# Moving the value-weight cluster, the logits and one eviction in a woven attention and expert kernel

## The chip, the cores and the metric

One core of a Trainium2 chip runs the whole program. The metric is device time in microseconds of one execution; the lower, the better. The profile shows five engines of the core: PE (TensorE, with its weight loads as PEld), DVE (VectorE), ACT (ScalarE), POOL (GpSimd) and SP (SyncE, which here only issues DMAs).

## The reference

Eight batches of eight heads with 576 tokens attend to 32 memory slots per head; the result goes through a mixture of eight experts of which each token uses one.

```
a = softmax(phi, over 32 slots)
k_m = a.T @ k ; v_m = a.T @ v                      per batch and head, 32 x 64
attn = softmax(q @ k_m.T / 8) ; x = attn @ v_m      4608 tokens x 512
logits = x @ w_gate + modality_bias[modality_id]
e = argmax(logits) ; gate = softmax(logits)[e]
out = gate * (relu(x @ w1[e]) @ w2[e])              w1 512 x 1024, w2 1024 x 512
```

## The kernel before, in words

The kernel guesses one expert for all tokens, computes with it, and at the end tests whether any token chose another; only then a general path runs. With the inputs here it doesn't run.

**What is computed per batch b (0 to 7).** `mem_max`, `mem_turn_top`, `mem_swap`, `mem_peak`, `mem_exp`, `mem_sums` (stages `max`, `ttop`, `swap`, `top`, `exp`, `sums`) make the softmax of `phi`; `kv_products` (stage `kv`, L388 and L396 on PE) the memory keys and values, `mem_turn` (stage `kvT`, L146) their transposes `kT` and `vT`. `q_turn` (stage `qt`, four DVE transposes, L552) turns the queries, `scores` (stage `s`, L564) multiplies them with `kT`; with it comes `mem_gate` (L541). `soften` and `normalise` (stages `e` and `n`, DVE with one ACT exp) make the attention weights in two parts, part 0 of 256 tokens and part 1 of 320, and transpose them into `aT`. `a_split` (stages `xu` on ACT and `x` on DVE) splits `aT` into a high and a low half, `xah`/`xal` and `xbh`/`xbl`. `logits` (stage `l`, L683 on PE, `lgT` and `lg` on DVE) and `gate` (stage `g`, L703 to L713 and one ACT exp) make `gates`.

**Value weights.** x @ w1 is never formed as such: `value_products` (L737) multiplies `vT` with the raw `w1`, and `split` (L151 on ACT, L152 on DVE) turns the product into the halves `vwh` and `vwl`. For batches 2 to 7 this is one cluster, `all_value_weights` (stage `vx`): 32 small matmuls into two banks named `pe` and two named `pair`, four casts, four subtractions.

**The two weight layers.** `hidden` (stage `h`, L794) is one of eight chunks f of the hidden layer for one part: six matmuls, then ACT writes `hh` (L807) and DVE `hl` (L811). `outputs` (stage `o`, L830) is one chunk f of one output tile of 128 tokens: three matmuls of 512 columns. Tiles 0 and 1 belong to part 0, tiles 2 and 3 to part 1, and every odd batch ends with a ninth tile for the last 64 tokens of both batches of a pair. After chunk 7, `store` has ACT scale the tile by `gates` into `ob` (L843) and SP store it.

**What sets the order.** Stages are put on two lists, `attention` and `experts`. Each carries its kind (whose cost on PE, DVE, ACT and POOL stands in the table `TAKES`), the stages it comes after, a due time and the PSUM banks it takes. `weave` walks both lists and emits the next attention stage when it is ready and due by the progress of the experts list, else the next expert stage. That order is final on each engine: nothing is reordered later. All tiles named `pe` share a ring of four PSUM banks, taken in turn; a matmul into a bank waits until its last user was read out. In the kernel before, the expert list holds `vx` of the next batch in the middle of the last tile of a batch, and `l` comes after the split of part 1.

Of the kernel before, what the change touches and what calls it, by code (L numbers as in the profile page):

```python
# [54 lines left out]
def attn_moe(ctx: ExitStack, tc: tile.TileContext, q, k, v, phi, mod_id, w_gate, mod_bias, w1, w2, out):  # L55
    nc = tc.nc
    B, H, S, D = q.shape
# [13 lines left out]
    FCH = FF // P  # L71
# [70 lines left out]
    live = {}  # L142
# [729 lines left out]
    def first_w2(c):  # L872
# [7 lines left out]
    attention, experts = [], []  # L880
# [20 lines left out]
    }  # L901


    WORTH = {"h": 0.35, "vw": 0.5, "vx": 0.5, "o": 1.0}
    BATCH = WORTH["h"] * FCH * (0.73 + 0.9) + 4.5 * FCH * 0.693 + WORTH["vw"] * 2.8

    def stage(to, name, kind, after, what, *args, due=-1.0, floor=0.0, banks=0, full=False):

        to.append((name, kind, after, due, floor, lambda: what(*args), banks, full))
# [113 lines left out]
    def plan_steps(b, dues):  # L1025

        free = [[("h", b - 2, part, FCH - 1)] if b > 1 else [] for part in range(2)]
        pair, i = b // 2, b % 2
        todo = []

        def add(name, kind, after, what, *args):
            todo.append((name, kind, after, what, args))

        def step(part):
            for k in range(4):
                before = ("e", b, part, k - 1) if k else ("s", b, part if b == 0 else 0)
                add(("e", b, part, k), f"e{part}{k}", [before], soften, b, part, k)

        def weights(part):
            for k in range(3):  # L1040
                before = [("n", b, part, k - 1) if k else ("e", b, part, 3)]
                if b and k == 2:
                    before += [("l", b - 1), ("x", b - 1, 1)]
                add(("n", b, part, k), f"n{part}{k}", before, normalise, b, part, k)

        def put(part):
            wait = free[part] + ([("w2", FCH - 1)] if b == 0 else [])
            add(("xu", b, part), f"xu{part}", [("n", b, part, 2)] + wait, a_split, b, part, 0)
            add(("x", b, part), f"xl{part}", [("xu", b, part)], a_split, b, part, 1)

        if b:
            add(("s", b, 0), "sg" if b > 1 else "s", [("kvT", b), ("qt", b, HG - 1)], scores_gate if b > 1 else scores, b)
            step(0)
            if b > 1:
                step(1)
            weights(0)
            put(0)
            if b == 1:
                step(1)
        else:  # L1060
            step(1)
            todo.insert(len(todo) - 1, (("vg", 0), "vg", [("e", 0, 1, 0)], mem_gate, (0,)))
        weights(1)
        if b == 0:
            put(1)
        if b < 2:
            add(("l", b), "l", [("n", b, 1, 2), ("vg", b)], logits, b)
        if b:
            put(1)
        if b > 1:  # L1070
            add(("l", b), "lx", [("n", b, 1, 2), ("vx", b)], logits, b)
        c0, n = RA * i, RB if i else RA
        add(("g", b), "g", [("l", b)], gate, pair, c0, n)
        if i:
            add(("others", pair), "others", [("g", b)], others, pair)
            if b < B - 1:
                add(("bias", pair + 1), "nothing", [], biases, pair + 1)
        for (name, kind, after, what, args), due in zip(todo, dues):
            one_bank = int(kind == "sg")
            stage(attention, name, kind, after, what, *args, due=due, banks=one_bank, full=bool(one_bank))  # L1080
        if b == B - 1:
            stage(attention, ("v",), "verdict", [("others", pair)], verdict, due=due + 12.0)

# [7 lines left out]
    def plan_experts(b):  # L1091
        def next_values(hf):
            if b + 1 < B:
                stage(experts, ("vw", b + 1, hf), "vw", [("kvT", b + 1)], value_weights, b + 1, hf, banks=2, full=True)

        def some(t, f, kind, terms):
            last_ = f == FCH - 1 and terms[-1] == 2
            stage(
                experts, ("o", b, t, f, terms[0]), ("o" if last_ else "") + kind, [("g", b)] if last_ else [],
                outputs, t, range(f, f + 1), store(b, t), terms, banks=int(f == terms[0] == 0), full=last_,  # L1100
            )

        def tile_(t):
            for f in range(FCH):
                some(t, f, "o", range(3))

                if b and t == (None if b % 2 else 3) and f == FCH // 2 - 1 and b + 1 < B:
                    stage(experts, ("vx", b + 1), "vw2", [("kvT", b + 1)], all_value_weights, b + 1, banks=2, full=True)
                if b == 0 and t == 3 and f == 1:
                    next_values(0)  # L1110
                if b == 0 and t == 3 and f == FCH - 1:
                    stage(experts, ("vwp", 1, 1), "vwpu", [("kvT", 1)], value_upper_weights, 1, 1, banks=2, full=True)
                    stage(experts, ("vw", 1, 1), "vwl", [("x", 1, 0), ("vwp", 1, 1)], value_lower, 1)
# [26 lines left out]
    def evenly(first, gap, n=24):  # L1140
        return [first + gap * k for k in range(n)]

    AHEAD, SPREAD = (5.8, 5.0), 0.55
    plan_first()
    plan_steps(0, evenly(1.4, 0.25))
    plan_memory(1, 5.9, floor=27.5)
    plan_turns(1, 10.0, 0.9, floor=36.7)
    plan_steps(1, evenly(16.5, 0.5, 10) + evenly(22.5, 0.4))
    for b in range(2, B):
        at0 = (b - 1) * BATCH - AHEAD[b > 2]  # L1150
        plan_memory(b, at0)
        plan_turns(b, at0 + 6.0, 1.3)
        plan_steps(b, evenly(at0 + 11.5, SPREAD, 24))
    for b in range(B):
        plan_experts(b)
    attention.sort(key=lambda s: s[3])
# [1 line left out]
    def weave():  # L1158
# [8 lines left out]
        def ready(s):  # L1167
            if not s or any(n not in done for n in s[0][2]):
                return None


            t = max([0.0] + [done[n] + (0.1 if n[0] != "sums" else -1.2) for n in s[0][2] if n[0] not in ("g", "vx")])
            pe, chain = TAKES[s[0][1]]
            if not pe and chain:

                t -= 0.3
                if t <= free["D" if chain[0] == "T" else chain[0]] or chain[0] == "P":
                    t = 0.0
            t = max(t, s[0][4])
            if s[0][6]:  # L1180
                t = max([t] + [ring[(turn_ + k) % 4] + 0.1 for k in range(s[0][6])])
            return t
# [196 lines left out]
```

## Time and profile before

| | us |
|---|---|
| median of 3 runs | 395.72 (395.28 to 395.73) |
| the profiled execution | 395.99 |
| its span, first to last instruction | 394.1 |
| PE busy | 378.3 (96%) |
| DVE busy | 244.8 (62%) |
| ACT busy | 143.1 (36%) |
| POOL busy | 46.3 (12%) |

The span is what the profile covers; the 1.9 us around it belong to the execution too. Matmuls are pipelined: a matmul of 256 columns shows some 0.28 us, but the next one starts 0.12 us after it, so PE's pace is read from starts, not from durations.

### The profile page before, as it was taken

How to read it: one execution, taken by the hardware profiler on the slowest of the kernel's cores; microseconds unless marked ns; L12 is line 12 of the kernel's file. 1: busy time of each engine (PE TensorE's matmuls, PEld its weight loads, DVE VectorE, ACT ScalarE, POOL GpSimd, SP SyncE). 2: the span in 40 equal slices, each digit the busy share in tenths (PEclk: the TensorE clock that was granted, in tenths of full speed). 3: DMA queues.
4: the chain of work that ended last, by engine and by line, in shares of the span. 5: the costliest groups of instructions: out<-in, count | busy, mean ns of one | idle time of the engine just before them, and what ended most of it. 6: DMA issues, size and time to landing. Idle time of an engine off the chain costs nothing.

```text
span 394.1 us, 10016 instructions
## 1 busy us (share of the span) xinstructions
PE 378.3 (96%) x4158; PEld 307.0 (78%) x4158; DVE 244.8 (62%) x620; ACT 143.1 (36%) x348; POOL 46.3 (12%) x113
## 2 busy tenths in 40 slices
PE   8799999999998999999999999999999999999992
PEld 3577885889767888788977879788887879688982
DVE  4787756895678467664867378674776558560400
ACT  2292524425134333423424333334424325431410
POOL 3247020023000300002000400002000300000000
PEclk9999999999999999999999999999999999999998
DMA  8999349435910493407520292423511011521121
GB/s 299 352 379 362 67 123 377 138 146 137 343 39 28 115 360 119 160 19 264 213 53 28 80 340 109 169 76 98 198 28 39 17 30 27 201 93 30 27 43 47
DMA packets 28844, 56.91 MB, mean 144 GB/s; under 512 B 3060, under 2 KB 8436, under 8 KB 28788
## 3 DMA queue, kind: packets, MB, share of 16 engines
q1 hardware_dynamic: 28368, 55.73, 42.6%
q8 instruction: 35, 0.57, 0.6%
q10 hardware_dynamic: 420, 0.43, 0.3%
q14 instruction: 21, 0.17, 0.1%
HBM read 37.28 MB, written 18.87 MB: 142 GB/s over the span
## 4 chain that ended last, share of the span: by engine, by line
PE 78%; DVE 12%; ACT 4%; DMA 3%; issue 1%; SPq 0%; ACTq 0%
PE pe L830 44%; PE pe L794 22%; PE pair L388 4%; DVE vwl L152 4%; PE pair L564 3%; DMA kv_sb<-in_v_dram 3%; PE pe L737 2%; ACT vwh L151 2%; ACT ob L843 1%; DVE xbl L666 1%; PE pair L737 1%; DVE lgT L690 1%; PE pair L146 1%; PE pe L413 1%; DVE a L603 0%
## 5 line engine op out<-in xcount | busy, mean ns | idle before, releaser
L830 PE MATMUL pe<-w2h,hh 128*128 128x512 f32 x288 | 115.4, 401 | 0.0
L830 PE MATMUL pe<-w2h,hl 128*128 128x512 f32 x288 | 112.4, 390 | 0.0
L830 PE MATMUL pe<-w2l,hh 128*128 128x512 f32 x288 | 110.2, 390 | 0.0
L811 DVE SCALAR_TENSOR_TENSOR hl<-pe,hh 128x256 fp32r<-128x256 f32 (+2 forms) x158 | 56.9, 391 | 30.1 <-ACT hh L807 27.0
L807 ACT ACTIVATE hh<-pe 128x256 fp32r<-128x256 f32 (+2 forms) x158 | 52.4, 363 | 39.8 <-PE pe L794 39.4
L830 PEld LDWEIGHTS pe<-w2h,hh 128*128 128x128 f32 x288 | 54.1, 188 | 12.7 <-issue 1.9
L830 PEld LDWEIGHTS pe<-w2l,hh 128*128 128x128 f32 x288 | 54.0, 188 | 11.7
L830 PEld LDWEIGHTS pe<-w2h,hl 128*128 128x128 f32 x288 | 54.1, 188 | 10.0
L843 ACT ACTIVATE ob<-pe,gates 128x512 f32<-128x512 f32 x35 | 24.0, 688 | 73.7 <-PE pe L830 36.3
L794 PE MATMUL pe<-xbh,vwh 128*128 128x320 f32 x128 | 40.3, 315 | 0.1
L794 PE MATMUL pe<-xah,vwh 128*128 128x256 f32 x124 | 36.2, 295 | 3.7 <-DVE hl L811 2.2
L794 PE MATMUL pe<-xbh,vwl 128*128 128x320 f32 x128 | 39.6, 309 | 0.0
L794 PE MATMUL pe<-xbl,vwh 128*128 128x320 f32 x128 | 39.5, 309 | 0.0
L794 PE MATMUL pe<-xal,vwh 128*128 128x256 f32 x124 | 34.9, 283 | 0.3 <-DVE xal L666 0.3
L794 PE MATMUL pe<-xah,vwl 128*128 128x256 f32 x124 | 34.8, 282 | 0.0
L322 POOL COPY ts<-tm 32x4 f32<-32x4 f32 x24 | 4.8, 200 | 212.2 <-DVE tm L314 211.5
L794 PEld LDWEIGHTS pe<-xah,vwh 128*128 128x128 f32 x124 | 23.6, 191 | 7.5 <-DVE hl L811 2.8
L794 PEld LDWEIGHTS pe<-xbh,vwh 128*128 128x128 f32 x128 | 24.0, 188 | 0.7 <-ACT ob L843 0.4
L794 PEld LDWEIGHTS pe<-xbl,vwh 128*128 128x128 f32 x128 | 24.0, 188 | 0.2
L794 PEld LDWEIGHTS pe<-xal,vwh 128*128 128x128 f32 x124 | 23.6, 191 | 0.8 <-DVE xal L666 0.5
L794 PEld LDWEIGHTS pe<-xbh,vwl 128*128 128x128 f32 x128 | 24.0, 188 | 0.0
L794 PEld LDWEIGHTS pe<-xah,vwl 128*128 128x128 f32 x124 | 23.6, 191 | 0.0
(178 smaller groups left out, 447.7 us busy)
## 6 DMA issues: line engine op xcount, KB each, us to landing
kv_sb<-in_k_dram SPq DMA_DIRECT2D x8, 1152.0 KB, 6.1
kv_sb<-in_v_dram SPq DMA_DIRECT2D x8, 1152.0 KB, 9.2
out_dram<-ob SPq DMA_DIRECT2D x65, 128.0 KB, 2.4
q_sb<-in_q_dram SPq DMA_DIRECT2D x7, 1152.0 KB, 7.9
ph<-in_phi_dram SPq DMA_DIRECT2D x7, 576.0 KB, 4.0
raw<-in_moe_w_dram SPq DMA_DIRECT2D x2, 1024.0 KB, 7.8
raw<-in_moe_w_dram SPq DMA_DIRECT2D x1, 1280.0 KB, 10.6
out_dram<-ob SPq DMA_DIRECT2D x3, 256.0 KB, 2.0
```

Source lines behind the costliest of these rows:

```text
L146: nc.tensor.transpose(dst, src, ident[:rows, :rows])
L151: nc.scalar.copy(h, src)
L152: nc.vector.tensor_tensor(l, src, h.bitcast(F32), op=ALU.subtract)
L322: nc.gpsimd.tensor_copy(ts_[BL * a:BL * (a + 1)], live["tm"][BL * o:BL * (o + 1)])
L388: nc.tensor.matmul(live["kvp"][M * j:M * (j + 1), g], lhsT=pe[half, j, c * M:(c + 1) * M], rhs=kv_sb[half, :, j, c * D:(c + 1) * D], start ...
L564: nc.tensor.matmul(sc[g][M * j:M * (j + 1), a, c0 * BL:(c0 + n) * BL].rearrange("p (c t) -> p c t", t=BL), lhsT=kTs[b % 2][p0:p0 + BL, u, ...
L737: nc.tensor.matmul(pvs[g][M * j:M * (j + 1), :], lhsT=vT[b][rows, j, :], rhs=raw1[rows, j, cols], start=True, stop=not more, tile_position ...
L794: nc.tensor.matmul(ph[:, 0:n], lhsT=(vl if k == 2 else vh)[:, g, cols], rhs=xl if k == 1 else xh, start=(g == k == 0), stop=(g == NG - 1 a ...
L807: nc.scalar.activation(hs[0][:, f, h0:h0 + p1 - p0], live["ph", f][:, p0:p1], AF.Relu)
L811: nc.vector.scalar_tensor_tensor(hl, live["ph", f][:, p0:p1], 0.0, hh.bitcast(F32), op0=ALU.max, op1=ALU.subtract)
L830: nc.tensor.matmul(po, lhsT=tile_columns(hl if n == 1 else hh, f, t), rhs=(w2l if n == 2 else w2h)[:, f, :], start=(f == n == 0), stop=(f ...
L843: nc.scalar.activation(ob, po, AF.Copy, scale=gate_of(b, t))
```

## The change

Five edits, all to the two lists; no instruction is added to the program that computes something new.

- `vx` of batch b (2 to 7) leaves the expert list. It is now an attention stage behind `n` of part 0 and ahead of the split of part 0, and it waits for the last `hidden` chunk of batch b - 1, whose weights it overwrites.
- `l` of batches 2 to 6 moves behind `exp` and `sums` of batch b + 1, and by its due time just ahead of `kv` of that batch; `g` follows `kv`. Batch 7 has no next batch and keeps `l` behind its split.
- The first output tile of batches 2 to 7 no longer waits for its gate when it ends: its bank is held, and the ACT eviction is a stage of its own (`late`) behind chunk 4 of the second tile.
- The planner's costs of `g`, `vx` and the new kind `late` change, and the due times of the batches: `BATCH` alternates for four and five tiles, and the constants of `plan_memory`, `plan_turns` and `plan_steps` are new.
- `max`, `ttop` and one `qt` thereby come earlier (below).

```diff
@@ -895,14 +895,18 @@
...
-    BATCH = WORTH["h"] * FCH * (0.73 + 0.9) + 4.5 * FCH * 0.693 + WORTH["vw"] * 2.8
+    BATCH = [WORTH["h"] * FCH * (0.73 + 0.9) + n * FCH * 0.693 for n in (4, 5)]
+
+    def begin(b):
+        return sum(BATCH[k % 2] for k in range(1, b)) + FIRST
+
@@ -1054,6 +1058,8 @@
             weights(0)
+            if b > 1:
+                add(("vx", b), "vw2", [("kvT", b), ("h", b - 1, 1, FCH - 1)], all_value_weights, b)
             put(0)
@@ -1068,16 +1074,19 @@
         if b > 1:
-            add(("l", b), "lx", [("n", b, 1, 2), ("vx", b)], logits, b)
+            add(("l", b), "lx", [("n", b, 1, 2), ("s", b, 0)] + ([("exp", b + 1), ("sums", b + 1)] if b + 1 < B else []), logits, b)
...
+        if 1 < b < B - 1:
+            at = [t[0][0] for t in todo].index("l")
+            dues = dues[:at] + [begin(b) - AHEAD[1] + MEMORY - 0.01] + evenly(begin(b) - AHEAD[1] + MEMORY + 0.01, 0.01, 8)
         for (name, kind, after, what, args), due in zip(todo, dues):
-            one_bank = int(kind == "sg")
-            stage(attention, name, kind, after, what, *args, due=due, banks=one_bank, full=bool(one_bank))
+            held = {"sg": 1, "vw2": 2}.get(kind, 0)
+            stage(attention, name, kind, after, what, *args, due=due, banks=held, full=bool(held))
@@ -1093,19 +1102,25 @@
+        late = b > 1
+
+        def hold(po):
+            live["late"] = lambda: store(b, 0)(po)
+
         def some(t, f, kind, terms):
             last_ = f == FCH - 1 and terms[-1] == 2
+            held = late and t == 0
             stage(
-                experts, ("o", b, t, f, terms[0]), ("o" if last_ else "") + kind, [("g", b)] if last_ else [],
-                outputs, t, range(f, f + 1), store(b, t), terms, banks=int(f == terms[0] == 0), full=last_,
+                experts, ("o", b, t, f, terms[0]), ("o" if last_ and not held else "") + kind, [("g", b)] if last_ and not held else [],
+                outputs, t, range(f, f + 1), hold if held else store(b, t), terms, banks=int(f == terms[0] == 0), full=last_ and not held,
             )
...
-                if b and t == (None if b % 2 else 3) and f == FCH // 2 - 1 and b + 1 < B:
-                    stage(experts, ("vx", b + 1), "vw2", [("kvT", b + 1)], all_value_weights, b + 1, banks=2, full=True)
+                if late and t == 1 and f == LATE:
+                    stage(experts, ("late", b), "late", [("g", b)], lambda: live.pop("late")())
@@ -1140,17 +1155,17 @@
-    AHEAD, SPREAD = (5.8, 5.0), 0.55
+    FIRST, AHEAD, SPREAD, MEMORY, LATE = 26.5, (1.4, 4.0), 0.55, 6.0, 4
...
-        at0 = (b - 1) * BATCH - AHEAD[b > 2]
+        at0 = begin(b - 1) - AHEAD[b > 2]
         plan_memory(b, at0)
-        plan_turns(b, at0 + 6.0, 1.3)
-        plan_steps(b, evenly(at0 + 11.5, SPREAD, 24))
+        plan_turns(b, at0 + 5.6, 1.0)
+        plan_steps(b, evenly(at0 + 9.5, SPREAD, 24))
```

Where this puts instructions is seen in the order on each engine. The first place is DVE ahead of the hidden layer of batch 4 (its `hl` rows of 128x256). Before, the four subtractions of the cluster (`vwl`), the whole gate (`lgT` to `gates`) and the maxima of batch 5 (`t2top`, `top`) stand between the split of part 1 (`xbl`) and the first `hl`:

```order
L629 STREAM_TRANSPOSE aT<-a 128x2x5x32 x2
L666 TENSOR_TENSOR xbl<-aT,xbh 128x640
L152 TENSOR_TENSOR vwl<-pe,vwh 128x512 x2
L152 TENSOR_TENSOR vwl<-pair_2847,vwh 128x512 x2
L690 STREAM_TRANSPOSE lgT<-pair_2864 128x128
...
L713 RECIPROCAL gates<-se 128x4
L279 TENSOR_TENSOR t2top<-ph_105 128x512
...
L283 TENSOR_TENSOR top<-top,ph_105 128x128
L811 SCALAR_TENSOR_TENSOR hl<-pe,hh 128x256 x4
L312 STREAM_TRANSPOSE tt<-top 128x128
```

In the changed kernel the same stretch of DVE reads:

```order
L629 STREAM_TRANSPOSE aT<-a 128x2x4x32 x2
L152 TENSOR_TENSOR vwl<-pe,vwh 128x512 x2
L152 TENSOR_TENSOR vwl<-pair_2783,vwh 128x512 x2
L666 TENSOR_TENSOR xal<-aT,xah 128x512
L613 TENSOR_REDUCE sa<-a 128x20
...
L666 TENSOR_TENSOR xbl<-aT,xbh 128x640
L279 TENSOR_TENSOR t2top<-ph_105 128x512
...
L332 STREAM_TRANSPOSE peaks<-tt 128x128
L811 SCALAR_TENSOR_TENSOR hl<-pe,hh 128x256 x8
L353 TENSOR_TENSOR exp<-ph_105,peaks 128x4x160
```

The cluster went up behind the transposes of part 0 (`aT` of 4x32), the gate left the stretch, and `ttop` and, in even batches, `top` came into it ahead of the first `hl`. In odd batches three `hl` stand ahead of the `top` rows.

The second place is DVE around the memory products of batch 5 (`den`, `rec` read their sums), up to the scores (`vg` and `a<-pair` follow them). Before:

```order
L353 TENSOR_TENSOR exp<-ph_105,peaks 128x4x128
L472 TENSOR_SCALAR den<-pair_3043 128x2
L474 RECIPROCAL rec<-den 128x2
L552 STREAM_TRANSPOSE q_sb_102<-q_sb_102 128x576 x4
L546 COPY vg_90<-pe 128x2x8
L597 STREAM_TRANSPOSE a<-pair_3162 128x256
```

In the changed kernel:

```order
L353 TENSOR_TENSOR exp<-ph_105,peaks 128x4x128
L552 STREAM_TRANSPOSE q_sb_102<-q_sb_102 128x576
L690 STREAM_TRANSPOSE lgT<-pair_3006 128x128
...
L472 TENSOR_SCALAR den<-pair_3025 128x2
L474 RECIPROCAL rec<-den 128x2
L703 TENSOR_REDUCE lm<-lg 128x4
...
L713 RECIPROCAL gates<-se 128x4
L552 STREAM_TRANSPOSE q_sb_102<-q_sb_102 128x576 x3
L546 COPY vg_90<-pe 128x2x8
```

The logits' DVE work now stands ahead of `den`, the gate between `rec` and the last three query transposes. On PE the logits of batch 4 and the products of batch 5 stand together there, seven chunks behind the hidden layer of batch 4; seven chunks (one of tile 0, six of tile 1) then stand between the products and the scores of batch 5, where it was five:

```order
L830 MATMUL pe<-w2l,hh 128x512
L683 MATMUL pair_3006<-aT,vg_90 32x128 x8
L683 MATMUL pair_3006<-aT,vg_90 32x32 x4
L388 MATMUL pair_3025<-kv_sb,exp 32x128 x72
L396 MATMUL pair_3025<-ones_c,sums 32x1 x8
L830 MATMUL pe<-w2h,hh 128x512
```

Before, `L683` followed `L737` there, and `L388` stood alone between chunks.

## Rows read from the trace of the kernel before

**Rows 1.** The page: span, and busy time of each engine.

```profile
span 394.1 us, 10016 instructions
PE 378.3 (96%) x4158; PEld 307.0 (78%) x4158; DVE 244.8 (62%) x620; ACT 143.1 (36%) x348; POOL 46.3 (12%) x113
```

**Rows 2.** Timeline of PE, hidden layers of batches 2, 3, 4: start, duration, [idle <-releaser].

```profile
121.29 0.28 PE L794 MATMUL pe<-xal,vwh 128*128 128x256 f32 x1
121.41 0.28 PE L794 MATMUL pe<-xah,vwl 128*128 128x256 f32 x1
121.90 0.39 PE L794 MATMUL pe<-xah,vwh 128*128 128x256 f32 x1 [0.21 <-ACT ob L843]
...
122.59 0.28 PE L794 MATMUL pe<-xah,vwl 128*128 128x256 f32 x1
124.01 0.39 PE L794 MATMUL pe<-xah,vwh 128*128 128x256 f32 x1 [1.14 <-DVE hl L811]
...
165.44 0.28 PE L794 MATMUL pe<-xah,vwl 128*128 128x256 f32 x1
166.01 0.38 PE L794 MATMUL pe<-xah,vwh 128*128 128x256 f32 x1 [0.30 <-ACT ob L843]
...
214.41 0.28 PE L794 MATMUL pe<-xah,vwl 128*128 128x256 f32 x1
215.21 0.38 PE L794 MATMUL pe<-xah,vwh 128*128 128x256 f32 x1 [0.51 <-DVE hl L811]
```

**Rows 3.** Timeline of PE around the value products and logits of batches 2 and 4.

```profile
113.40 0.39 PE L830 MATMUL pe<-w2l,hh 128*128 128x512 f32 x1
...
115.60 0.50 PE L830 MATMUL pe<-w2h,hh 128*128 128x512 f32 x1
...
117.17 0.50 PE L830 MATMUL pe<-w2h,hh 128*128 128x512 f32 x1
...
205.92 0.39 PE L830 MATMUL pe<-w2l,hh 128*128 128x512 f32 x1
...
208.80 0.50 PE L830 MATMUL pe<-w2h,hh 128*128 128x512 f32 x1
```

**Rows 4.** The chain that ended last, batch 4's tiles 2 and 3: start, us, what.

```profile
241.05 8.18 PE pe L830 x36
```

**Rows 5.** Busy time by stretches: stretch, length, PE, PEld, DVE, ACT, POOL, PE clock, DMA.

```profile
103.41:110.88 7.47, 7.47 (x33) 6.17 (x34) 7.19 (x15) 1.95 (x3) 0.00 (x0) 1.00 0.64 211
108.18:110.88 2.70, 2.70 (x13) 2.25 (x12) 2.56 (x7) 0.74 (x1) 0.00 (x0) 1.00 0.23 62
116.06:119.25 3.19, 3.19 (x36) 2.42 (x35) 2.54 (x6) 1.62 (x3) 0.00 (x0) 1.00 0.02 5
112.39:116.13 3.74, 3.74 (x41) 1.79 (x40) 3.60 (x8) 1.23 (x3) 0.00 (x0) 1.00 0.33 70
204.26:205.83 1.57, 1.57 (x9) 1.30 (x8) 0.82 (x1) 0.72 (x2) 0.00 (x0) 1.00 0.19 42
262.10:264.55 2.45, 2.45 (x13) 2.02 (x12) 2.28 (x7) 0.00 (x0) 0.00 (x0) 1.00 0.00 0
192.68:199.03 6.35, 6.35 (x30) 5.23 (x29) 5.84 (x14) 1.93 (x4) 0.00 (x0) 1.00 0.02 7
211.19:213.13 1.94, 1.94 (x16) 1.84 (x15) 1.77 (x13) 0.93 (x3) 0.00 (x0) 1.00 0.00 0
```

**Rows 6.** Timeline of DVE, ACT and PE from batch 5's memory products to its splits.

```profile
226.22 0.16 DVE L472 TENSOR_SCALAR den<-pair 128x2 f32<-128x2 f32 x1 [5.67 <-PE pair L396]
226.50 2.73 DVE L552 STREAM_TRANSPOSE q_sb<-q_sb 128x576 f32<-128x576 f32 x4
...
227.19 0.52 ACT L482 ACTIVATE values<-pair,rec 128x64 f32<-128x64 f32 x2
...
229.95 1.60 PE L564 MATMUL pair<-q_sb,kT 32*32 32x288 f32 x64
...
241.35 0.82 DVE L811 SCALAR_TENSOR_TENSOR hl<-pe,hh 128x320 fp32r<-128x320 f32 x2
```

More of the change, by code (lines that the diff above doesn't have):

```diff
@@ L1169, in ready @@
                 return None
-            t = max([0.0] + [done[n] + (0.1 if n[0] != "sums" else -1.2) for n in s[0][2] if n[0] not in ("g", "vx")])
+            t = max([0.0] + [done[n] + (0.1 if n[0] != "sums" else -1.2) for n in s[0][2] if n[0] != "g"])
             pe, chain = TAKES[s[0][1]]
```

4 rows, old and new, of the table TAKES are left out of this document.

## The prediction

> **What bounds the kernel now.** I read the page first, then the chain that ended last, then the timeline of PE stretch by stretch. The page says PE: it is busy for 378.3 of 394.1 us, and no other engine for more than two thirds [rows 1]. The table of stretches gives its clock as 1.00 everywhere in the batches [rows 5], so the upper of its two levels, 2.4 GHz. The change alters no matmul, so it can only win the time in which PE stands still inside the batches, and lose by making new stops. The loads at the start and the last tile's store at the end stay as they are.
>
> The stops are found by comparing starts. Inside a hidden chunk the matmuls start 0.12 us apart (121.29 to 121.41). Where a chunk starts late, the row's bracket names who released it: ACT's `ob` or DVE's `hl` [rows 2]. Less the regular 0.12, batch 2 loses 0.37 (121.41 to 121.90) and 1.30 (122.59 to 124.01), batch 3 0.45 (165.44 to 166.01), batch 4 0.68 (214.41 to 215.21). Batches 5 and 7 repeat batch 3 with 0.45 each, batch 6 repeats batch 4 with 0.67. That is seven stops in six hidden layers, together **4.37 us**, all in part 0, two to four chunks after its start.
>
> Why they are there: a hidden chunk needs a free bank of the ring of four. In batches 4 and 6 DVE still works on the cluster's subtractions, the gate and the maxima when the first chunks end, so `hl` is late and the fifth chunk waits. In batches 3, 5 and 7 the last tile waits on ACT for the exp and the gate of the same late chain (`ob`), and the chunk that wants that tile's bank waits. The cause is DVE work packed between `vx` and the first `hl`.
>
> **The change, part by part.** All of it goes by DVE's and PE's positions in order, so I add up both up to the first hidden layer. Prices are stretches of DVE work that the trace has in one piece, with pauses [rows 5]: `normalise` of part 0, 2.70; the four subtractions with the pause before the last, 3.19; from the start of `xal` to the end of part 1's transposes, 3.74; `xbh` on ACT and `xbl`, 1.57; maxima and `ttop`, 2.45. PE's: a chunk of outputs is 3 x 8.18/36 = 0.68 [rows 4]; the cluster of value products is 1.97 (113.40 to 115.60, less one regular step of 0.23) [rows 3]; a hidden chunk of part 0 is 0.72, six steps.
>
> *Odd batches (3, 5; batch 7 has no maxima).* Count from the first chunk of tile 2 of the batch before, 241.05 for batch 5 [rows 4]. There DVE finishes its last two `hl` at 242.17, 1.1 later [rows 6]. In the changed order an exp stands on ACT ahead of the last `hh`, so I allow 1.35. Then 2.70 + 3.19 + 3.74 + 1.57 + 2.45 = 13.65, so DVE is free for the first `hl` at 15.0 and has done it at 15.4. PE does 16 chunks (10.9) and the cluster (2.0), starts the hidden layer at 12.9, and asks for that bank after four chunks, at 15.8. Margin 0.4: no stop. The gate is gone from ACT's way, too, and the tile that waited for it has its gate a whole tile earlier.
>
> *Even batches (4, 6).* Part 0 is normalised 6.35 after the start of tile 2 [rows 5]; 3.19 + 3.74 + 1.57 + 2.45 make 17.3, and `top`, which waits for POOL, I bound by the price of maxima and `ttop` once more, 2.45: 19.8, first `hl` done at 20.2. PE has 24 chunks and the cluster, 18.4, and asks at 21.3. Margin 1.1.
>
> *Batch 2.* DVE is busy without a break from the scores to `aT` of part 0, 103.41 to 110.88 [rows 5]. The scores come one chunk sooner, so 110.2; plus 3.19, 3.74, 1.57 and 2.45 is 121.1, first `hl` released at 121.6. PE's hidden layer, at 119.4 before, starts 1.0 earlier without the logits, at 118.4, and asks at 121.3. A stop of **0.2 to 0.3** stays; bounds 0 and the old 1.67, and I take the sum.
>
> *Re-entries.* PE's steps after another kind of matmul are slower, and the trace has the cluster and the logits both joined and apart [rows 3]. Joined they cost 205.92 to 208.80 less 0.23, 2.65. Apart, 1.97 and, from 115.60 to 117.17 less the three output matmuls (0.34 + 0.23 + 0.23), 0.77: with one more slow entry of 0.11 it is 2.85. Logits directly ahead of the memory products, as now in batches 2 to 6, are not in the trace; they share one re-entry with them, so they lie between: 0 to 0.2 more per batch for 3 to 6, up to 0.2 less for batch 2, 0.2 more for 7. I take **0.4** in all; bounds 0 and 1.0.
>
> *The gate between `rec` and the query transposes.* This is the edit's own new risk, since DVE's transposes release the scores. `den` is at 226.22 [rows 6]; the gate follows, and its exp stands on ACT behind keys and values, which end at 227.71 [rows 6]; the whole logits and gate work is 1.94 long [rows 5], so the gates are done at 228.6 at the latest. Three transposes are 2.05 (2.73 x 3/4) [rows 6]: 230.7. The scores were at 229.95 [rows 6] and come two chunks later, 231.3. Margin 0.6: nothing. In even batches one more chunk lies between, and 0.4 of DVE work (`others`): margin 0.9.
>
> *Free edits.* The held bank costs nothing: tile 0's bank is wanted again by the second hidden chunk of part 1, after three more chunks of tile 1 and the scores. ACT reaches `late` behind `vT`, when the gates exist. The cluster's two banks and the pair are free: their users are `hl` of the batch before and transposes that stand ahead of part 0's `normalise`. Without this cover each would cost PE what it lacks, one for one. The products stand as far behind exp and sums as in even batches before: seven chunks and the logits, 5.5, in place of eight chunks. SP's loads keep their places next to the products. The verdict moves up six chunks and may cost 0.1, since its DVE step queues behind the last `hl`.
>
> *Sum.* 4.37 - 0.25 - 0.4 - 0.1 = 3.6 gained. From the profiled execution's 395.99 that is 392.4; it lies 0.27 above the median of 395.72, so against the median **392.1**.
>
> **The rivals.** *DVE stays late.* For it: my margins in odd batches are 0.4 in 15, every piece was timed in other company, and the order is strict: what stands in front of `hl` delays it. Against it: 1.9 of gate work left the stretch. If odd batches 3, 5 and 7 keep 0.45 and batch 2 keeps 0.8, 1.9 less is won: **394.0**. The Trainium skill (TensorE: Matmul & The Clock Gate, Architectural detail) says that VectorE and ScalarE take their queues strictly first in, first out. By that rule the pause inside the four subtractions delays all behind it, which is why I priced that stretch with its pause; the trace agrees, as `hl` waits behind the maxima.
>
> *The stops only move.* If the planner's new due times push about as much waiting to the scores or to part 1, the time is **395.5**. Against it: those places have no stop now and the sums above leave room.
>
> *Slower: the scores behind the gate.* Place: the last query transpose, five times (batches 3 to 7). It decides once DVE ends it more than 0.6 to 0.9 later than I summed; then PE stands still one for one, and the hidden chunks of part 1 come late behind it. To end above the old time it needs some 3.6/5 = 0.7 beyond the margin, 1.5 later in all. For it: the gate hangs on an ACT exp behind four copies. At 1.9 late, five times 1.2 are lost against 3.6: **398**.
>
> *No effect at all*, the order unchanged, is excluded by the rows in the section on the change.
>
> **How the numbers follow.** Nearly all stops gone: 0.64, 391.2 to 393.2, at 392.1. DVE stays late: 0.19, 393.2 to 394.8. Stops only move: 0.08, about 395.5. Slower: 0.09, 396.6 to 399. The low end has 0.9 beyond the sum: no residual stop and no re-entries, 391.3, a little rounding. The range from 391.0 to 394.7 takes in the first two, 0.83. A measurement of this kernel can tell 0.2%, 0.8 us, from no change; faster than that is 0.83, within it 0.08, slower 0.09.
>
> **What would show it.** In the changed profile PE's row for L794 should have no start more than 0.3 us late in part 0 of batches 3 to 7, and at most a small one on `hl` in batch 2. `vwl` should stand two tiles ahead of the hidden layer, and ACT's `ob` should no longer release a hidden chunk. The scores (L564) and the memory products should start within a step of the chunk before them. PE's busy time stays at 378 while the span falls. I am wrong if a wait on `q_sb`, `hl` or `sums` of over 0.3 us recurs in every batch, or if PE's own steps around the logits and products grow by more than 1 us in all.

## The result, and the profile after

The changed kernel takes **389.81 us** (median of 4 runs, 388.99 to 390.58), the kernel before on the same chip 395.50 (395.14 to 395.73): ratio 0.9857, 95% interval 0.9832 to 0.9881. A second measurement on another chip, the first of the experiments below, gave 390.15 against 395.79, ratio 0.9856 (0.9841 to 0.9871). So the change wins 5.6 to 5.7 us where 3.6 were forecast, and the time lies 1.2 below the low end of the range. The profiled execution took 390.23, its span is 388.4.

The page of the changed kernel, to be held against [rows 1], with the chain's shares by engine:

```profile
span 388.4 us, 10022 instructions
PE 375.2 (97%) x4157; PEld 306.2 (79%) x4158; DVE 247.9 (64%) x620; ACT 143.8 (37%) x348; POOL 46.1 (12%) x113
...
PE 91%; DMA 3%; DVE 3%; ACT 1%; issue 1%; SPq 0%; ACTq 0%
```

The span fell by 5.7, PE's busy time by 3.1. The forecast had said that busy time stays at 378; it doesn't, since a matmul's row (0.28) is longer than its step (0.12), so that part of every stop counts as busy, and the slow step behind it does too.

The chain that ended last, the hidden layers of part 0 in batches 4 to 7 (start, us, what, matmuls):

```profile
208.28 5.75 PE pe L794 x48
...
250.42 5.75 PE pe L794 x48
...
298.00 5.75 PE pe L794 x48
...
341.06 5.75 PE pe L794 x48
```

Each is one piece of 48 matmuls without a break. The timeline of PE in the changed kernel, first at the place in batch 5 where the kernel before stopped, then the one stop that is left, in batch 2:

```profile
253.01 0.28 PE L794 MATMUL pe<-xah,vwl 128*128 128x256 f32 x1
253.13 0.28 PE L794 MATMUL pe<-xah,vwh 128*128 128x256 f32 x1
253.25 0.28 PE L794 MATMUL pe<-xal,vwh 128*128 128x256 f32 x1
...
121.01 0.28 PE L794 MATMUL pe<-xah,vwl 128*128 128x256 f32 x1
121.19 0.39 PE L794 MATMUL pe<-xah,vwh 128*128 128x256 f32 x1
121.41 0.28 PE L794 MATMUL pe<-xal,vwh 128*128 128x256 f32 x1
```

The fifth chunk of batch 5 starts 0.12 behind the matmul before it, like any other. In batch 2 it starts 0.18 behind, and the step after that is 0.22.

To see where time is lost in all, I took for each matmul the step from its start to the next start, less the median step of its kind, and summed this from 70 us on by what stands before and behind (one profiled execution of each):

| excess of PE's steps, us | before | changed |
|---|---|---|
| inside hidden layers (L794 to L794) | 6.03 | 0.20 |
| going into and out of value products, logits and memory products (L737, L683, L388, L396) | 5.63 | 5.63 |
| between output matmuls (L830 to L830) | 3.13 | 3.45 |
| inside the scores (L564 to L564) | 1.17 | 1.54 |

The last row differs only by the median that is taken off (16 ns in one trace, 15 in the other): the 378 steps inside the scores sum to 7.21 in both.

In the six hidden layers of part 0 alone the excess was 1.85, 0.71, 0.76, 0.73, 0.75 and 0.73, together 5.53, and is 0.14 now, all in batch 2. The last matmul starts 5.63 sooner (386.70 to 381.07); 5.39 of that are these layers.

### The profile page after: what moved, and what is told of

Same layout as the page of the kernel before. It is cut to its first block, busy times and chain, and to the rows that moved or that the text cites. A ratio compares the mean times of both kernels' runs of the same rounds, so it can differ in the third digit from the quotient of the medians.

```text
span 388.4 us, 10022 instructions
## 1 busy us (share of the span) xinstructions
PE 375.2 (97%) x4157; PEld 306.2 (79%) x4158; DVE 247.9 (64%) x620; ACT 143.8 (37%) x348; POOL 46.1 (12%) x113
## 4 chain that ended last, share of the span: by engine, by line
PE 91%; DMA 3%; DVE 3%; ACT 1%; issue 1%; SPq 0%; ACTq 0%
PE pe L830 50%; PE pe L794 26%; PE pair L388 4%; PE pair L564 3%; DMA kv_sb<-in_v_dram 3%; PE pe L737 2%; PE pair L737 2%; PE pair L683 1%; PE pair L146 1%; PE pe L413 1%; DVE a L603 0%; PE pair L794 0%; ACT ob L843 0%; PE pe L541 0%; PE pair L396 0%
## 5 line engine op out<-in xcount | busy, mean ns | idle before, releaser
L830 PE MATMUL pe<-w2h,hh 128*128 128x512 f32 x288 | 115.7, 402 | 0.0
L830 PE MATMUL pe<-w2h,hl 128*128 128x512 f32 x288 | 112.5, 391 | 0.0
L830 PE MATMUL pe<-w2l,hh 128*128 128x512 f32 x288 | 110.1, 390 | 0.0
L811 DVE SCALAR_TENSOR_TENSOR hl<-pe,hh 128x256 fp32r<-128x256 f32 (+2 forms) x158 | 58.1, 392 | 37.5 <-ACT hh L807 36.8
L830 PEld LDWEIGHTS pe<-w2h,hh 128*128 128x128 f32 x288 | 54.0, 188 | 16.6 <-ACT vwh L151 4.2
L807 ACT ACTIVATE hh<-pe 128x256 fp32r<-128x256 f32 (+2 forms) x158 | 53.3, 362 | 36.7 <-PE pe L794 36.4
L830 PEld LDWEIGHTS pe<-w2l,hh 128*128 128x128 f32 x288 | 54.0, 188 | 11.7
L830 PEld LDWEIGHTS pe<-w2h,hl 128*128 128x128 f32 x288 | 54.1, 188 | 9.7
L794 PE MATMUL pe<-xbh,vwh 128*128 128x320 f32 x128 | 39.9, 311 | 0.1
L794 PE MATMUL pe<-xbh,vwl 128*128 128x320 f32 x128 | 39.5, 309 | 0.0
L794 PE MATMUL pe<-xbl,vwh 128*128 128x320 f32 x128 | 39.5, 309 | 0.0
L794 PE MATMUL pe<-xah,vwh 128*128 128x256 f32 x124 | 35.3, 288 | 0.4 <-ACT xah L663 0.4
L794 PE MATMUL pe<-xal,vwh 128*128 128x256 f32 x124 | 35.0, 284 | 0.3 <-DVE xal L666 0.3
L794 PE MATMUL pe<-xah,vwl 128*128 128x256 f32 x124 | 34.9, 283 | 0.0
L794 PEld LDWEIGHTS pe<-xah,vwh 128*128 128x128 f32 x124 | 23.7, 191 | 2.5 <-ACT xah L663 1.3
L794 PEld LDWEIGHTS pe<-xbh,vwh 128*128 128x128 f32 x128 | 24.0, 188 | 0.8 <-ACT ob L843 0.3
L794 PEld LDWEIGHTS pe<-xbl,vwh 128*128 128x128 f32 x128 | 24.0, 188 | 0.3
L794 PEld LDWEIGHTS pe<-xal,vwh 128*128 128x128 f32 x124 | 23.7, 192 | 0.8 <-DVE xal L666 0.5
L794 PEld LDWEIGHTS pe<-xbh,vwl 128*128 128x128 f32 x128 | 24.0, 188 | 0.0
L794 PEld LDWEIGHTS pe<-xah,vwl 128*128 128x128 f32 x124 | 23.7, 191 | 0.0
```

What stands on the lines that cost most here:

```text
L794: nc.tensor.matmul(ph[:, 0:n], lhsT=(vl if k == 2 else vh)[:, g, cols], rhs=xl if k == 1 else xh, start=(g == k == 0), stop=(g == NG - 1 a ...
L807: nc.scalar.activation(hs[0][:, f, h0:h0 + p1 - p0], live["ph", f][:, p0:p1], AF.Relu)
L811: nc.vector.scalar_tensor_tensor(hl, live["ph", f][:, p0:p1], 0.0, hh.bitcast(F32), op0=ALU.max, op1=ALU.subtract)
L830: nc.tensor.matmul(po, lhsT=tile_columns(hl if n == 1 else hh, f, t), rhs=(w2l if n == 2 else w2h)[:, f, :], start=(f == n == 0), stop=(f ...
```

## The experiments

All but the repeat write the order of stages down before it is emitted and move single stages in it, or put additions into it, so that the planner does not shift anything else:

```diff
-            s[5]()
+            order.append(s)
...
+        def move(name, behind):
+            s = order.pop([x[0] for x in order].index(name))
+            order.insert([x[0] for x in order].index(behind) + 1, s)
...
+        for s in order:
+            s[5]()
```

In the three kernels that start from the one before, a last argument of 0 puts the stage ahead of the one named instead of behind it.

| kernel | median us | ratio to before (95%) |
|---|---|---|
| changed, repeated | 390.15 | 0.9856 (0.9841 to 0.9871) |
| before, cluster alone moved | 401.05 | 1.0126 (1.0106 to 1.0146) |
| before, logits and gate alone moved | 391.48 | 0.9894 (0.9879 to 0.9909) |
| before, cluster moved, logits later | 396.04 | 1.0025 (1.0011 to 1.0040) |
| changed, cluster back | 395.26 | 0.9990 (0.9981 to 0.9999) |
| changed, logits and gate back | 395.51 | 0.9996 (0.9986 to 1.0007) |
| changed, no hold | 390.04 | 0.9859 (0.9843 to 0.9876) |
| changed, 3 additions before `hl` | 395.93 | 1.0005 (0.9994 to 1.0016) |
| changed, 3 additions before the transposes | 393.98 | 0.9960 (0.9946 to 0.9974) |
| changed, 5 additions before `hl` | 406.79 | 1.0301 (1.0262 to 1.0340) |

**The changed kernel again.**

> The changed kernel once more, on one chip with the next three. Both theories: 389.8, between 389.0 and 390.6. Hidden layers of part 0 (48 matmuls from first to the one behind) at 5.75 us in batches 3 to 7, PE's first step after any stop absent.

390.15, with the five hidden layers at 5.75. The differences below are taken against this run or against the kernel before, 395.79 beside this run and the three others on its chip, and 395.04 to 395.68 beside the later ones.

**The cluster alone.** Two theories stood against each other. "Packed queue" is the prediction's: gate work in front of `hl` makes the stops. "Late cluster" came from reading the trace of the kernel before again, where DVE is not packed all through that stretch (in batches 3 to 7). These are its timeline rows of DVE in batches 4 and 5, where it stands idle for 2.20 and 2.95 before its first `vwl`:

```profile
208.04 1.29 DVE L152 TENSOR_TENSOR vwl<-pe,vwh 128x512 fp32r<-128x512 f32 x2 [2.20 <-ACT vwh L151]
...
250.96 1.29 DVE L152 TENSOR_TENSOR vwl<-pe,vwh 128x512 fp32r<-128x512 f32 x2 [2.95 <-ACT vwh L151]
```

```diff
+        for b in range(2, B):
+            move(("vx", b), ("xu", b, 0), 0)
```

> The kernel before with the cluster of value products alone moved ahead of the split of part 0; logits, gate, due times and eviction as before. Theory 'late cluster': in the kernel before, VectorE stood idle 2.95 us (batch 5) and 2.20 us (batch 4) ahead of its first vwl, waiting for the cluster; with the cluster earlier this idle time goes, the gates come 2 us sooner in odd batches and hl 4 us sooner in even ones, so the stops of batches 3 to 7 go; batch 2, where VectorE had no such idle time ahead of vwl, keeps about 1.0. Time about 391.2. Theory 'packed queue' (the one of the prediction: it is the 1.94 us of gate work in front of hl that makes the stops, wherever the cluster stands): the stops stay, 395.

Both were wrong about the time: 401.05, 5.3 slower than before. The stops in the hidden layers did go (5.75 in batches 3 to 7), and another wait came in their place. The waits of PE in this kernel (us in total, times, longest), and its timeline in batch 3:

```profile
PE pair L683 <- DVE aT L629: 7.0, 4, 2.8
...
161.63 0.39 PE L830 MATMUL pe<-w2l,hh 128*128 128x512 f32 x1
163.42 0.94 PE L683 MATMUL pair<-aT,vg 128*32 128x128 f32 x24 [1.41 <-DVE aT L629]
```

The logits stood where they were on PE, but the `aT` of part 1 that they read now came later on DVE, behind the four subtractions (in batch 2 at 118.86, 116.13 before). They waited in batches 2, 3, 5 and 7, 7.7 us by the steps. Only batches 4 and 6, where PE waited for nothing, show that the earlier cluster by itself takes a stop away there; in the other four PE's own wait of 1.6 to 2.9 stood ahead of the hidden layer and gave DVE that much more time. The Trainium skill (TensorE: Matmul & The Clock Gate, Architectural detail) has VectorE take its queue strictly first in, first out; this run agrees, as the subtractions and `xal` (111.98 to 115.73 in batch 2) stand in front of the sums and transposes of part 1 (to 118.86). The wait in batch 2 was followed by 3.2 us at half the clock (last section), 1.6 lost, and the logits behind each wait took 0.17 longer (0.93 or 0.94 in place of 0.76), 0.7. With 5.2 of stops gone that makes 7.7 + 1.6 + 0.7 - 5.2 = 4.8 of the 5.3.

**Logits and gate alone.** The other half, moved as in the change, only that the gate stands two or three query transposes later than there; the due times stay the old ones. The hold must come with it, since the gate is later than the first tile's end.

```diff
+        for b in range(2, B - 1):
+            move(("qt", b + 1, 0), ("kv", b + 1), 0)
+            move(("l", b), ("kv", b + 1), 0)
+            move(("g", b), ("qt", b + 1, 3 - b % 2))
...
+            at = max(names.index(n) for n in (("o", b, 1, 4, 0), ("kvT", b + 1), ("g", b)) if n in names)
+            order.insert(at + 1, ((), "", [], 0, 0, lambda: live.pop("late")()))
```

> The kernel before with logits and gate alone moved to the memory products of the next batch (one query transpose with them, and the first tile's eviction held, which the later gate needs); the cluster stays in the middle of the last tile. Packed queue: 1.94 us less in front of hl, all stops but a rest of 0.5 in batch 2 go, about 391.0. Late cluster: in odd batches it was the gate behind the idle time that was waited for, and that is gone too, and in even batches hl comes 1.9 sooner, so the same 391; only if the cluster's place were the sole cause would even batches keep 0.6 each and the time be 393.

391.48, 4.3 of the 5.6 us. The timeline of PE has two stops left, in batch 2 (`hl`) and in batch 7 (`ob`, where logits and gate did not move and the old chain is intact):

```profile
119.88 0.28 PE L794 MATMUL pe<-xah,vwl 128*128 128x256 f32 x1
120.79 0.39 PE L794 MATMUL pe<-xah,vwh 128*128 128x256 f32 x1 [0.63 <-DVE hl L811]
...
342.54 0.28 PE L794 MATMUL pe<-xah,vwl 128*128 128x256 f32 x1
343.12 0.39 PE L794 MATMUL pe<-xah,vwh 128*128 128x256 f32 x1 [0.30 <-ACT ob L843]
```

So most of the gain is this part's. The cluster's place, with the new due times, is worth 1.3 on top of it: it takes away the excess of those two layers, 0.87 and 0.71, but for 0.14.

**The cluster alone, with the logits out of its way.** To see whether the logits' wait was the whole loss, they go directly ahead of the hidden layer in the four batches that waited.

```diff
+        for b in (2, 3, 5, 7):
+            move(("l", b), ("h", b, 0, 0), 0)
+            move(("g", b), ("h", b, 0, 0), 0)
...
```

> The kernel before with the cluster moved ahead of the split of part 0 as in the run of the cluster alone, and in batches 2, 3, 5 and 7, where TensorE stood 1.6 to 2.9 us at the logits there, logits and gate put directly ahead of the hidden layer. If that run was slow only because its logits waited for part 1's aT, the four waits of 7.64 go, 401.05 - 7.64 = 393.4; the gate now stands closer to hl, so from its timeline batch 2 stops 1.2 and the odd batches 0.3 each, with slow first steps 2.5 in all: 395 to 396, about the kernel before, and the row of L683 has no wait over 0.3. If the cluster's earlier place costs something else (a bank, ScalarE's casts), the time stays over 398.

396.04, 0.7 above the kernel before on its chip (395.32): the four waits fall to one of 0.73, and the time comes back nearly to that of the kernel before, as expected. It does not get better, because the gate now stands between the late `aT` and `hl`: the odd batches stop for 0.42 each and batch 2 for 2.12, 0.9 more than I had summed. In the profiled execution (397.49) the clock is 0.51 from 125.7 to 129.0 behind that stop.

**The cluster back.**

```diff
+        for b in range(2, B):
+            move(("vx", b), ("o", b - 1, None if b % 2 == 0 else 3, FCH // 2 - 1, 0))
```

> The changed kernel with the cluster alone put back into the middle of the last tile, everything else in the changed order. Late cluster: from the cluster's start to the end of vwl are 4.94 us (239.41 to 244.35 in the changed kernel), then xbl 0.75 and maxima with ttop 2.45 stand in front of hl: it comes 0.8 late in batches 3 and 5, 2.8 late in 4 and 6 (there top stands in front as well), 0.9 in batch 2, none in 7; with 0.10 for each slow first step 8.6 in all, 398.4, slower than the kernel before. Packed queue: VectorE's work in front of hl is the same sum as in the changed kernel, so nothing changes, 389.8 to 390.5.

395.26, so 5.1 of the gain is gone, though not the 8.6 of the forecast; the stops make 3.8 of it (excess inside hidden layers 3.95 against 0.19). The timeline of DVE, then of PE, in batch 3:

```profile
159.00 1.29 DVE L152 TENSOR_TENSOR vwl<-pe,vwh 128x512 fp32r<-128x512 f32 x2 [1.73 <-ACT vwh L151]
...
165.29 1.08 DVE L811 SCALAR_TENSOR_TENSOR hl<-pe,hh 128x256 fp32r<-128x256 f32 x3
...
164.69 0.28 PE L794 MATMUL pe<-xah,vwl 128*128 128x256 f32 x1
165.76 0.38 PE L794 MATMUL pe<-xah,vwh 128*128 128x256 f32 x1 [0.80 <-DVE hl L811]
```

Batches 2, 3 and 5 stop for 0.95 each, as summed (0.8 to 0.9). Batches 4 and 6 hardly stop (none and 0.11): in the changed order maxima stand ahead of `vwl` there and fill the time in which DVE waits for the cluster. That was the error in the 8.6. Batch 7, forecast at none, stops for 0.26 and a second small time, 0.5 in all. In the profiled execution the memory products also stood still three times, 2.0 us in all more than in the repeat, for nothing that the profile shows; why is open, and that execution (396.39) is one of the slowest of the kernel.

The late cluster is not the whole cause here. It stands in the same place in the run with logits and gate alone moved, which took 391.48, 3.8 less. The timeline of DVE in batch 3, first in that run, then in this one:

```profile
160.34 0.82 DVE L666 TENSOR_TENSOR xbl<-aT,xbh 128x640 fp32r<-128x640 f32 x1
161.51 0.42 DVE L811 SCALAR_TENSOR_TENSOR hl<-pe,hh 128x256 fp32r<-128x256 f32 x1 [0.35 <-ACT hh L807]
...
162.17 0.83 DVE L666 TENSOR_TENSOR xbl<-aT,xbh 128x640 fp32r<-128x640 f32 x1
162.91 0.68 DVE L279 TENSOR_TENSOR t2top<-ph 128x512 f32<-128x512 f32 x1
```

With the old due times `hl` follows `xbl` and has to wait for `hh`; batches 3 and 5 don't stop. The planner's new due times and costs put the maxima of the next batch, from `t2top` at 162.91 on, in front of the first `hl` at 165.29 here; in odd batches of the kernel before they stand behind the eighth. In the changed kernel, with the cluster early, there is room for those 2.4 us.

**Logits and gate back.**

```diff
+        for b in range(2, B - 1):
+            move(("l", b), ("x", b, 1))
+            move(("g", b), ("l", b))
...
```

> The changed kernel with logits and gate alone put back behind the split of part 1, everything else in the changed order. There part 1's aT is ready before TensorE reaches the logits (248.0 against 248.9 in batch 5 of the changed kernel), so unlike in the run with the cluster alone the logits wait for nothing; but the gate's 1.94 us stands in front of maxima and hl again, and the hidden layer starts only 0.65 later. From the margins of the changed kernel (odd 0.7, even 1.1, batch 2 none): stops of 0.6 in batches 3 and 5, 0.2 in 4 and 6, 1.3 in batch 2, none new in 7, and 0.10 for each slow first step: 3.4 in all, 393.5. Rival, that after the joined and earlier cluster the gate's place no longer matters: 390.2.

395.51, 5.4 slower than the repeat. Timeline of DVE, then PE, in batch 5:

```profile
253.42 0.57 DVE L690 STREAM_TRANSPOSE lgT<-pair 128x128 f32<-128x128 f32 x2
...
256.01 0.16 DVE L719 TENSOR_REDUCE badp<-other 128x1 f32<-128x9 f32 x1
256.09 0.68 DVE L279 TENSOR_TENSOR t2top<-ph 128x512 f32<-128x512 f32 x1
...
257.55 0.28 PE L794 MATMUL pe<-xah,vwl 128*128 128x256 f32 x1
259.07 0.38 PE L794 MATMUL pe<-xah,vwh 128*128 128x256 f32 x1 [1.24 <-DVE hl L811]
```

The mechanism is the one expected: the gate is back in front of maxima and `hl`, and the fifth chunk starts 1.40 late, as it does in batch 3; batch 2 stops for 1.22, near the 1.3 of the forecast, and batches 4 and 6 not at all. The size was off for two reasons. In an odd batch the stretch is 2.67 (253.42 to 256.09, with `others` and a fifth column), not 1.94. And logits that share no re-entry with another kind of matmul cost more: the steps into and out of such groups sum to 6.09 in place of 5.63, those between output matmuls to 4.20 in place of 3.48, 1.2 us together. The stops are 4.2 of the 5.4 (excess inside hidden layers 4.38 against 0.19).

In the changed order, then, either half put back makes DVE late for `hl` again. But there the maxima stand in front of `hl`, too; with the old due times the logits and gate moved alone kept 4.3 of the 5.6, and the cluster moved alone lost.

**No hold.**

```diff
+        for b in range(2, B):
+            move(("late", b), ("o", b, 0, FCH - 1, 0))
```

> The changed kernel with the first tile's eviction at the tile's end again, where it waits for its gate; everything else in the changed order. If the hold is only insurance: ScalarE stands on the gate some 1 to 2 us, kT and vT come behind it, and the scores, which had 0.9 to 1.2 to spare, start at most 0.3 later: 390.2 to 391. If the hold carries part of the gain: kT comes over 1 us late for the scores in five batches, 394 or more.

390.04, no difference. Timeline of ACT behind batch 4's tile 0:

```profile
224.55 0.69 ACT L843 ACTIVATE ob<-pe,gates 128x512 f32<-128x512 f32 x1 [0.80 <-PE pair L146]
225.13 0.36 ACT L514 COPY kT<-pair 128x256 f32<-128x256 f32 x1
```

`kT` is done at 225.49, and the scores start at 227.24. The hold protects only a margin that is not used.

**Three additions in front of `hl`.** This measures the margin, and what a stop of known length costs.

```diff
+            if s[0][:1] == ("h",) and s[0][1] > 2 and s[0][2:] == (0, 0):
+                for k in range(3):
+                    nc.vector.tensor_tensor(fill, fill, fill, op=ALU.add)
```

> The changed kernel with three additions of 128x512 on VectorE (0.60 each from start to start, 1.8) put directly in front of the first hl of batches 3 to 7; they compute nothing that is used. Margins read in the changed kernel: first hl done at 162.7 and its bank asked for at 163.4 in batch 3 (0.7, the same in 5), 1.1 in 4 and 6 with 0.2 of waiting for hh, 1.05 in 7. So stops of 1.1, 0.5, 1.1, 0.5, 0.8: 4.0. If a stop costs only what stands in its bracket: 394.2. If the first step behind a stop is slow as well (0.22 in place of 0.12), and in odd batches a second small one: 394.7 or a little more, with a step of 0.22 in each hidden layer of part 0. With the margins of the prediction (0.4 and 1.1) it would be 394.6 and 395.1.

395.93, 5.8 more. Timeline of DVE, then PE, in batch 3:

```profile
162.19 2.13 DVE L1243 TENSOR_TENSOR fill<-fill 128x512 f32<-128x512 f32 x3
164.24 1.08 DVE L811 SCALAR_TENSOR_TENSOR hl<-pe,hh 128x256 fp32r<-128x256 f32 x3
...
163.20 0.28 PE L794 MATMUL pe<-xah,vwl 128*128 128x256 f32 x1
164.72 0.39 PE L794 MATMUL pe<-xah,vwh 128*128 128x256 f32 x1 [1.24 <-DVE hl L811]
164.94 0.28 PE L794 MATMUL pe<-xal,vwh 128*128 128x256 f32 x1
```

Each addition reads what the one before it wrote, and they start 0.72 apart where the independent `vwl` start 0.6 apart; the three take 2.05 (162.19 to 164.24), not 1.8. With 2.05 the forecast gaps are 1.35, 0.75, 1.35, 0.75 and 1.0, together 5.2; measured are 1.40, 0.68, 1.40, 0.68 and 1.07, together 5.23. The margins were read rightly, with the 0.2 of waiting for `hh` in batches 4 and 6 beside them. The excess inside the hidden layers is 5.74 above the repeat, 0.5 more than the gaps: behind every one of the five stops a step of 0.22 stands in place of 0.12 (164.72 to 164.94). No second small stop came.

**Three additions in front of the transposes**, the same lines at `qt` 1 of batches 3 to 7, the place of the rival "slower".

> The changed kernel with the same three additions (1.8) between the gate and the last three query transposes of batches 3 to 7, as a test of the margin of the scores, the place of the rival 'slower'. Read in the changed kernel: last transpose done at 136.41, scores start at 137.29, 0.9 in batches 3, 5 and 7; 178.92 and 180.12, 1.2 in 4 and 6. So the scores come 0.95 late three times and 0.65 late twice: 4.2, 394.4 to 394.8. By the prediction's margins of 0.6 and 0.9: 395.8. If something else than the transposes released the scores (kT): 390.2.

393.98, 3.8 more. Timeline of PE's weight loads in batch 3:

```profile
137.55 0.18 PEld L564 LDWEIGHTS pair<-q_sb,kT 32*32 32x32 f32 x16 [0.35 <-issue]
138.14 0.15 PEld L564 LDWEIGHTS pair<-q_sb,kT 32*32 32x32 f32 x8 [0.41 <-DVE q_sb L552]
138.80 0.86 PEld L564 LDWEIGHTS pair<-q_sb,kT 32*32 32x32 f32 x40 [0.51 <-DVE q_sb L552]
```

The scores wait for the transposes, as that rival has it, and stretch from 1.53 to 2.58, 2.24, 2.57, 2.24 and 2.54, 4.5 us in all. A fill of 2.05 less margins of 0.9 and 1.2 makes 1.15 and 0.85 each, 5.15; measured are 1.04 and 0.71. So the margin is about 1.0 in batches 3, 5 and 7 and 1.3 in 4 and 6, and the median time lost is less than the profiled execution's (394.93, the slowest of five).

**Five additions in front of `hl`**, after two runs had shown a slow clock behind a long stop.

> The changed kernel with five additions in front of the first hl of batches 3 to 7, in place of three (0.68 each by the run with three, 3.42 in all). By the margins of that run (2.05 of fill gave start gaps 1.40, 0.68, 1.40, 0.68, 1.07 too long) the gaps are now 2.77, 2.05, 2.77, 2.05, 2.44 too long: 12.1, with 0.10 for each slow first step 12.6: 402.7. If a stop as long as that is followed by a stretch at the lower clock, as behind the stops of 2.1 and 3.0 in two earlier runs (16 steps of 0.21 in place of 0.12, 1.5), each batch loses 1.5 more: 410, with a granted clock of 0.50 for some 3 us in each hidden layer of part 0.

406.79, between the two numbers, with runs from 403.83 (mean granted clock 0.993) to 409.35 (0.978). The stretches of this kernel, PE alone (stretch, length, PE, granted clock, DMA), behind the stops of batches 3, 4, 6 and 7:

```profile
165.60:169.00 3.40, 3.40 (x26) 1.00 0.02 5
...
215.40:219.00 3.60, 3.60 (x27) 1.00 0.02 5
...
310.65:313.80 3.15, 3.15 (x16) 0.50 0.00 0
...
358.40:361.60 3.20, 3.20 (x18) 0.50 0.00 0
```

The gaps are 2.86, 2.13, 2.86, 2.13 and 2.52, 12.5 together and near the forecast. Behind three of the five stops the clock stays at 1.00, behind two it falls to 0.50.

## Why the prediction was right in direction and too small

Right were the place of the loss, the sign and, in the main, the mechanism: seven stops in part 0's hidden layers vanish but for a rest in batch 2. Against the sum of 3.6 (4.37 - 0.25 - 0.4 - 0.1) the profile has these terms.

- **The stops: 4.37 taken, 5.53 measured. This is the step that failed.** I priced a stop by the start that it delays, "Less the regular 0.12", and stopped reading there. The step behind that start is slow too: 0.22 or 0.23 in place of 0.12, seven times, 0.7. And in batches 3, 5 and 7 a second small stop follows three steps later, with its own slow step, 0.18 a batch, 0.5. Both stand in the trace of the kernel before, right behind the rows that I quoted; its timeline of PE in batch 3, going on from [rows 2]:

```profile
166.24 0.28 PE L794 MATMUL pe<-xal,vwh 128*128 128x256 f32 x1
...
166.71 0.28 PE L794 MATMUL pe<-xah,vwl 128*128 128x256 f32 x1
166.91 0.38 PE L794 MATMUL pe<-xah,vwh 128*128 128x256 f32 x1
167.13 0.28 PE L794 MATMUL pe<-xal,vwh 128*128 128x256 f32 x1
```

  166.01 to 166.24 is 0.23, 166.71 to 166.91 0.20, 166.91 to 167.13 0.22. Had I compared the lengths of whole layers (254.59 to 261.08 in batch 5 of the kernel before, 6.49, against 48 x 0.12 = 5.76), the term would have been right. The run with three additions shows the slow step behind stops made on purpose, each time 0.10.
- **Re-entries: 0.4 taken, 0.0 measured** (5.63 both times). Logits joined with the memory products save in batches 3 to 6 just what they saved with the cluster. The lower bound of 0 was the true value. That re-entries are a real cost the run with the logits back shows, where logits that share none cost 1.2 more.
- **Rest in batch 2: 0.25 taken, 0.14 measured** (0.05 and a slow step).
- **Verdict: 0.1 taken, nothing measured**: from the last matmul's start to the end it is 7.4 in both.

Together 5.53 - 0.14 = 5.39 in place of 3.6; the other 0.2 to 0.3 of the 5.6 to 5.7 lie outside these layers and are not traced to a term. The range's low end (no rest, no re-entries) left 4.37 as it was, and so could not reach 390.

**Margins.** For `hl` I had 0.4 in odd batches and 1.1 in even ones; in the changed profile they are 0.7 and 1.1, and the additions confirm it (0.65 and 1.2). For the scores I had 0.6 and 0.9; they are 0.9 and 1.2 by the timeline, 1.0 and 1.3 by the additions. So "slower" was a real mechanism (its place did stop PE once delayed), with 0.3 to 0.4 more room than I gave it.

**The cause, as the prediction put it, was half of it.** "DVE work packed between `vx` and the first `hl`" overlooks that in batches 3 to 7 DVE stood idle for 2 to 3 us in that very stretch, waiting for the cluster. Shown by the runs: the gate's removal alone wins 4.3 and takes every stop out of batches 3 to 6; the cluster's move alone loses 5.3, since it pushes part 1's `aT` behind the logits that need it; given the moved logits, the cluster's move and the due times together win the last 1.3. The hold costs and wins nothing, as said.

The prediction priced the maxima in front of `hl` (2.45 of its 13.65) without saying that in batches 3 and 5 the new due times put them there. With the cluster late and the logits moved, the new order takes 3.8 more than the old one (395.26 against 391.48); 2.3 of that are stops in the hidden layers of part 0 (excess 3.83 against 1.54), the rest is open. So the 5.1 that the cluster's move is worth in the changed order is not what it is worth by itself. Not run is the changed kernel with the old due times; whether the new ones win anything is open.

## What to carry to other kernels

Price a stop by the length of the whole stretch against the same stretch without one, not by the late start alone; here that was a fifth of the gain. When a stage moves ahead on an in-order engine, ask at once which later stage's input it pushes back: the cluster was right only once the logits behind it had left. And edits that travel together can need each other: here one alone brought most of the gain, one alone lost, and new due times were a loss without the earlier cluster. Run each alone, and name the one that was not, before giving any the credit.

## What was not expected of the hardware

After a stop PE's first step is slow, 0.22 in place of 0.12 for 256 columns, however long the stop (gaps of 0.05 to 2.9 us too long), with the granted clock at 1.00.

Some stops were also followed by a stretch at the lower of the clock's two levels, 1.2 GHz. In the run with the cluster alone, batch 2, PE resumed at 118.52 after 2.9 us, ran until 120.2 at 1.00 and then at half that. The stretches of that kernel (as above):

```profile
115.40:118.50 3.10, 0.35 (x2) 1.00 0.00 0
118.50:120.20 1.70, 1.68 (x28) 1.00 0.00 0
120.20:123.40 3.20, 3.20 (x11) 0.50 0.02 5
```

There a matmul of 256 columns starts 0.21 after the last, one of 512 columns 0.43. It lasted at least that row's 3.2 us; with five additions, 16 steps of 0.21 in place of 0.12 cost batch 6 1.5 us beyond its stop. The length of the stop alone did not decide: gaps 2.13 too long left the clock at 1.00 in batch 4 of that kernel and were followed by 0.50 in batch 6, and behind 2.86 in batch 3 it stayed at 1.00. Gaps of up to 1.4 (three additions, logits back) and batch 2's 1.3 in the kernel before were not followed by it. Nor did it come in every execution of one kernel, it seems: with the cluster moved and the logits later (stop of 2.12 in batch 2), five of twelve executions have a mean granted clock of 0.991 or 0.992 and take 396.80 to 397.74, the other seven 0.994 to 0.996 and 394.95 to 396.09. What tells the cases apart was not tried.
